# Sixteen attention units: a loop with a fixed body replaced by one written-out order of all calls

## The chip, the core and the metric

The kernel runs on one core of one Trainium2 chip. The core has five engines with a queue each: TensorE (PE, matrix products and transposes), VectorE (DVE), ScalarE (ACT), GpSimd (POOL) and SyncE (SP), which issues all DMAs here. An engine works through its own queue in order and stops where an instruction waits for another engine. The metric is device microseconds (us) of one execution; lower is better. Times below are medians of repeated runs, and one more execution was profiled.

## The reference

Three parts follow each other. (a) A linear attention with decay over B=4 batches, H=8 heads, 768 tokens and head size 48. (b) A soft mixture of experts (MoE) over all 3072 tokens. (c) A feed-forward network (FFN) with squared relu.

```python
for t in range(S):
    kt, vt, rt = (k[:, :, t], v[:, :, t], r[:, :, t])
    cur = np.einsum('bhd,bhe->bhde', u[None] * kt, vt)
    y[:, :, t] = np.einsum('bhd,bhde->bhe', rt, state + cur)
    state = w[None, :, :, None] * state + np.einsum('bhd,bhe->bhde', kt, vt)
...
logits = x @ phi                       # 3072 tokens, 8 experts x 4 slots
d = softmax over tokens of logits;  c = softmax over slots of logits
slot_input = d.T @ x                   # then per expert relu(. @ w1[e]) @ w2[e]
x = c @ slot_out
...
h = x @ w_in;  out = maximum(h, 0)**2 @ w_out     # 384 -> 2048 -> 384
```

## The kernel before

The attention is cut into 16 units n: batch b = n//4 and two heads of it. A unit holds 768 tokens as six chunks of 128, handled by parity (`par`, three even and three odd chunks). Its data come in one DMA (`load_unit`, L88) into one of five slots of SBUF. All calls are Python functions that issue a handful of instructions; a manual schedule keeps them in the order written, so the order of the calls is the order in each engine's queue. For unit n:

- `decay(n, m)` (VectorE, L236) multiplies the loaded r (m=0) or k (m=1) by powers of the decay.
- `turns(x, k)` (TensorE, L269) transposes 24 small blocks: the result of unit x back to token layout and the k of unit k. ScalarE copies both out (L266 to L276).
- `pr1` (L280), `pr2` (L284), `weigh` (VectorE, L288) and `diag(n, par)` (GpSimd, L295) make the diagonal term; `diag` writes a tile AT, of which there are three.
- `A(n, par)` (TensorE, L306): six products into two PSUM banks, one for each head. Three banks carry the tag "A"; `both` (L395, softmax transposes) and `soft3` (L446) take one of the three as well. `cp(n, par)` (VectorE, two instructions at L311) copies the two banks under a mask into AT and so frees them.
- `KV(n)` (TensorE, L318), `scan(n)` (VectorE, L322), `inter(n)` (TensorE, L336) and `intra(n, par)` (TensorE, L345) finish the unit. ScalarE copies each parity's result to a tile xT (L348), which `L(n)` (TensorE, L359) multiplies with phi.
- Per batch, softmax calls run beside later units: `soft1a` to `soft1d`, `both`, `c_max`, `c_sub` (GpSimd, L407), `c_exp`, `c_sum`, `c_div` (GpSimd, L419), `soft3`, and `soft4` (VectorE, L456). Tiles `nat` (written by `both`), `pb` (by `soft3`) and `sm` (by `c_sum`) exist once each.

Units 0 to 3 are written out by hand; units 4 to 15 run through one loop body. On TensorE the body's order is A(n,1), turns(n-1,n+2), in every fourth turn both, A(n+1,0), L(n-1), in every fourth soft3, inter(n), KV(n+1), intra(n,0), intra(n,1). The weight pieces of the MoE (24 of 512 KB, then larger ones) are issued by SyncE at the end of each turn. `keep_clock` and `filler` are products without use that keep TensorE at work in the first 13 us. After unit 15 come the last softmax steps (L686 to L727), the MoE (L743 to L783) and 96 equal steps of the FFN (L1023 the largest part); none of these is touched.

Of the kernel before, what the change touches and what calls it, by code (L numbers as in the profile page):

```python
# [17 lines left out]
def rwkv_softmoe_ffn(ctx: ExitStack, tc: tile.TileContext, un, wt, ph, w1, w2, w_in, w_out, out):  # L18
# [160 lines left out]
    def load_weight(i, cs=None):  # L179
        kind, e = W[i]  # L180
        if W[i] not in wt_of:
            t = take(home[i])
            wt_of[W[i]] = t.rearrange("p (c f) -> p c f", c=3) if kind == "w1" else t.rearrange("p (c d) -> p c d", c=8)
            st["raw", i] = t.rearrange("p (c f) -> p c f", c=3)
        t = st["raw", i]
        src = w1[e].rearrange("(c p) f -> c p f", p=128) if kind == "w1" else w2[e]
        if cs is None:
            nc.sync.dma_start(t, src.rearrange("c p f -> p c f"))
        else:
            for c in cs:  # L190
                nc.sync.dma_start(t[:, c], src[c])
# [217 lines left out]
    def c_exp(b):  # L409
        nc.scalar.activation(cnat[:, b], cnat[:, b], AF.Exp)  # L410
# [30 lines left out]
    def soft3(b, tag="A"):  # L441
        en = st["en", b]
        p = ps(tag)
        for h in range(2):
            for g in range(3):
                nc.tensor.matmul(p[32 * g:32 * g + 32, :DM + 1], en[:, h, 32 * g:32 * g + 32],  # L446
                                 xn[b % 2][:, 2 * g + h], start=(h == 0), stop=(h == 1))
        if b == 0:
            nc.scalar.copy(P2[:, 0], p[:96, :DM + 1])
        else:  # L450
            st["pb"] = wk([96, DM + 1], "pb", 1)
            nc.scalar.activation(st["pb"], p[:96, :DM + 1], AF.Copy, scale=st["f", b][1])
# [97 lines left out]
    intra(0, 1)  # L550
    rk(2)
    UT_of()
    A(1, 1)
# [12 lines left out]
    decay(3, 0)
    intra(1, 0)
    pr1(4)
    KV(2)
    intra(1, 1)  # L570
    scan(2)
    load_next(1)
    L(0)
    turns(0, 3)
    decay(4, 1)
    pr2(3)
    A(2, 0)
# [23 lines left out]
    pr2(4)
    intra(3, 0)
    decay(5, 0)
    cp(3, 1)
    KV(4)
    weigh(4)
    intra(3, 1)
    load_next(3)
    decay(6, 1)
    diag(4, 0)  # L610
    pr2(5)
    cp(4, 0)
    diag(4, 1)
    scan(4)
    for n in range(N0, NU):
        nxt = n + 1 < NU
        nx2 = n + 2 < NU
        nx3 = n + 3 < NU
        prev = n // NP - 1
        hp = n % NP  # L620
        if n == 7:
            sel = const.tile([128, 4, NS], F32, name="sel")
            nc.vector.reduce_sum(sel, ident.rearrange("p (q s) -> p s q", q=4).unsqueeze(1).to_broadcast([128, 4, NS, 4]), axis=AX.X)
            rm = const.tile([128, E], F32, name="rm")
            nc.vector.reduce_sum(rm, ident.rearrange("p (q e j) -> p e q j", q=4, e=E), axis=AX.XY)
            ones = const.tile([1, 4], F32, name="ones")
            nc.gpsimd.memset(ones, 1.0)
        A(n, 1)
        if prev >= 0 and hp == 2:
            c_exp(prev)  # L630
        if nx2:
            pr1(n + 2)
        if nxt:
            weigh(n + 1)
            diag(n + 1, 0)
        cp(n, 1)
        if prev >= 0 and hp == 2:
            c_sum(prev)
        if n > 0 or nx2:
            turns(n - 1 if n > 0 else None, n + 2 if nx2 else None)  # L640
        if prev >= 0 and hp == 1:
            both(prev)
            soft1d(prev)
        if nx2:
            pr2(n + 2)
        if nx3:
            decay(n + 3, 1)
        if nxt:
# [4 lines left out]
        if prev >= 0 and hp == 2:
            soft3(prev)
        if prev >= 0 and hp == 0:
            soft1a(prev)
            soft1c(prev)
        if prev >= 0 and hp == 1:
            c_max(prev)
        if nxt:  # L660
            diag(n + 1, 1)
        inter(n)
        if nxt:
            KV(n + 1)
        if nx2:
            decay(n + 2, 0)
        if nxt:
            scan(n + 1)
        intra(n, 0)
        if prev >= 0 and hp == 0:  # L670
            soft1b(prev)
        intra(n, 1)
        if prev >= 0 and hp == 1:
            c_sub(prev)
        if prev >= 0 and hp == 2:
            c_div(prev)
            soft4(prev)
        load_next(n)
        if n + NB >= NU:
            if n == NU - 2:  # L680
                load_win(0, take(NSLOT, I32))
            if n == NU - 1:
                load_weight(NSLOT)
            load_weight(NEARLY + n - NL)
# [410 lines left out]
```

## Time and profile before

| what | value |
|---|---|
| median of 3 runs | 379.99 us (379.57 to 380.36) |
| the profiled execution | 380.17 us, of which the span is 378.5 us |
| TensorE busy in the span | 368.8 us, 97% |
| VectorE, ScalarE, GpSimd busy | 266.6, 203.9, 106.6 us |
| stages | start and units to 115.2 us, softmax tail to 121.7, MoE to 154.1, FFN to 378.5 |

A busy row covers the time from an instruction's first work to its modelled end; a row of TensorE that stands on several products ("x12") can hold short waits between them, so an engine that is busy for 97% can still be waiting inside such rows. The idle time in front of a row stands in brackets with what ended it.

### The profile page before, as it was taken

How to read it: one execution, taken by the hardware profiler on the slowest of the kernel's cores; microseconds unless marked ns; L12 is line 12 of the kernel's file. 1: busy time of each engine (PE TensorE's matmuls, PEld its weight loads, DVE VectorE, ACT ScalarE, POOL GpSimd, SP SyncE). 2: the span in 40 equal slices, each digit the busy share in tenths (PEclk: the TensorE clock that was granted, in tenths of full speed). 3: DMA queues.
4: the chain of work that ended last, by engine and by line, in shares of the span. 5: the costliest groups of instructions: out<-in, count | busy, mean ns of one | idle time of the engine just before them, and what ended most of it. 6: DMA issues, size and time to landing. Idle time of an engine off the chain costs nothing.

```text
span 378.5 us, 9041 instructions
## 1 busy us (share of the span) xinstructions
PE 368.8 (97%) x3705; PEld 298.6 (79%) x3705; DVE 266.6 (70%) x460; ACT 203.9 (54%) x438; POOL 106.6 (28%) x118
## 2 busy tenths in 40 slices
PE   7999999999999999999999999999999999999995
PEld 6878878888877555888888888888888878888884
DVE  7777889999853486799876767666566756656662
ACT  2234444544532342899787856555555555555553
POOL 4765876768732131255121500000000000000000
PEclk9999999999999999999999999999999999999999
DMA  7999798998999998334232004000000120000004
GB/s 248 409 415 405 270 365 309 353 343 333 409 341 413 416 418 305 116 99 133 79 112 66 11 0 166 3 0 0 2 1 0 57 112 0 2 1 0 2 0 167
DMA packets 22281, 65.09 MB, mean 172 GB/s; under 512 B 2416, under 2 KB 4448, under 8 KB 22240
## 3 DMA queue, kind: packets, MB, share of 16 engines
q1 hardware_dynamic: 22240, 64.52, 45.2%
q8 instruction: 29, 0.48, 0.5%
q14 instruction: 12, 0.10, 0.1%
HBM read 59.00 MB, written 4.72 MB: 168 GB/s over the span
## 4 chain that ended last, share of the span: by engine, by line
PE 91%; DVE 5%; DMA 2%; ACT 1%; issue 1%; ACTq 0%; DVEq 0%
PE ps_A L1023 25%; PE ps_Y L1023 9%; PE ps_kv L1023 8%; PE ps_lg L1023 8%; PE ps_A L306 7%; PE ps_tr L928 6%; PE ps_YO L336 3%; PE ps_A L743 3%; PE ps_YE L345 3%; PE ps_Y L764 3%; PE ps_YO L345 3%; PE ps_kv L318 2%; PE ps_lg L359 2%; DVE AT L311 1%; DMA out_dram<-slot 1%; PE ps_YE L269 1%
## 5 line engine op out<-in xcount | busy, mean ns | idle before, releaser
L952 DVE TENSOR_TENSOR slot<-slot,slot 128x512 fp32r<-128x512 f32 (+1 forms) x97 | 69.5, 718 | 53.3 <-ACT slot L949 18.5
L1023 PE MATMUL ps_A<-slot,slot 128*128 128x512 f32 x432 | 105.8, 389 | 0.0
L1023 PEld LDWEIGHTS ps_A<-slot,slot 128*128 128x128 f32 x432 | 81.0, 188 | 17.1 <-ACT slot L949 0.3
L949 ACT CAST slot<-slot 128x512 fp32r<-128x512 f32 (+1 forms) x97 | 59.7, 616 | 49.9 <-DVE slot L946 49.6
L939 ACT ACTIVATE slot<-ps_tr 128x512 f32<-128x512 f32 (+1 forms) x97 | 57.4, 593 | 21.8 <-PE ps_tr L928 21.0
L946 DVE TENSOR_TENSOR slot<-slot 128x512 f32<-128x512 f32 (+1 forms) x71 | 48.4, 683 | 10.7 <-ACT slot L939 10.4
L1023 PE MATMUL ps_Y<-slot,slot 128*128 128x512 f32 x144 | 55.5, 392 | 0.2 <-ACT slot L949 0.2
L1023 PE MATMUL ps_kv<-slot,slot 128*128 128x512 f32 x144 | 55.1, 389 | 0.0
L1023 PE MATMUL ps_lg<-slot,slot 128*128 128x512 f32 x144 | 55.1, 389 | 0.0
L311 DVE COPY_PREDICATED AT<-mask,ps_A 128x384 f32<-128x384 int32 x63 | 33.6, 586 | 12.9 <-PE ps_A L306 7.9
L928 PE MATMUL ps_tr<-slot,slot 128*128 128x512 f32 x96 | 37.4, 391 | 0.4 <-DVE slot L892 0.4
L808 POOL TENSOR_TENSOR slot<-wf,slot 128x384 fp32r<-128x384 f32 x16 | 22.3, 1394 | 51.6 <-ACT slot L803 51.6
L295 POOL TENSOR_SCALAR_AFFINE_SELECT AT<-dg 128x768 f32<-128x768 f32 x32 | 28.1, 884 | 23.8 <-PE ps_YE L345 13.4
L306 PE MATMUL ps_A<-slot 48*128 48x128 f32 x378 | 33.3, 289 | 1.2 <-DVE AT L311 1.0
L1023 PEld LDWEIGHTS ps_Y<-slot,slot 128*128 128x128 f32 x144 | 27.0, 188 | 6.5 <-ACT slot L949 0.6
L1023 PEld LDWEIGHTS ps_kv<-slot,slot 128*128 128x128 f32 x144 | 27.0, 188 | 5.7
L306 PEld LDWEIGHTS ps_A<-slot 48*128 48x128 f32 x378 | 27.3, 188 | 5.2 <-DVE AT L311 2.2
L1023 PEld LDWEIGHTS ps_lg<-slot,slot 128*128 128x128 f32 x144 | 27.0, 188 | 5.5
L236 DVE TENSOR_TENSOR slot<-slot,ps_tab 112x768 f32<-112x768 f32 (+1 forms) x34 | 29.9, 891 | 1.0 <-DMA slot<-in_un_dram 1.0
L348 ACT COPY xT<-ps_YE 112x384 f32<-112x384 f32 x16 | 7.7, 480 | 30.6 <-PE ps_YE L345 30.6
L928 PEld LDWEIGHTS ps_tr<-slot,slot 128*128 128x128 f32 x96 | 17.9, 188 | 4.2 <-DVE slot L892 0.6
L284 POOL TENSOR_TENSOR slot<-slot,slot 128x576 f32<-128x576 f32 x13 | 18.4, 1417 | 7.4 <-ACT slot L276 7.1
(208 smaller groups left out, 531.4 us busy)
## 6 DMA issues: line engine op xcount, KB each, us to landing
slot<-in_un_dram SPq DMA_DIRECT2D x12, 1344.0 KB, 7.1
slot<-in_w_dram SPq DMA_DIRECT2D x24, 512.0 KB, 9.3
slot<-in_w_dram SPq DMA_DIRECT2D x8, 1536.0 KB, 10.5
slot<-in_w_in_dram SPq DMA_DIRECT2D x4, 1536.0 KB, 9.3
wo<-in_w_out_dram SPq DMA_DIRECT2D x16, 384.0 KB, 3.2
out_dram<-slot SPq DMA_DIRECT2D x18, 256.0 KB, 2.1
slot<-in_un_dram SPq DMA_DIRECT2D x9, 448.0 KB, 7.3
slot<-slot SPq DMA_DIRECT2D x48, 16.0 KB, 1.9
```

The lines of the kernel that those rows point to most:

```text
L236: nc.vector.tensor_tensor(x, x, t.unsqueeze(1).to_broadcast(list(x.shape)), ALU.mult)
L295: nc.gpsimd.affine_select(out=at, in_=dg.unsqueeze(3).to_broadcast([128, 2, HC, 128]), pattern=[[0, 2], [0, HC], [1, 128]], compare_op=ALU ...
L306: nc.tensor.matmul(p[h][:, i], tv[rows, 1, 2 * i + par], tv[rows, 0, 2 * i + par], start=True, stop=True)
L311: nc.vector.copy_predicated(st[n, "AT", par][:, h], mask.unsqueeze(1).to_broadcast([128, HC, 128]), p)
L345: nc.tensor.matmul(p[o:o + D, i], vv[:, 2 * i + par, h], at[:, h, i], start=False, stop=True, skip_group_check=True)
L808: nc.gpsimd.tensor_tensor(wout_half(wls, f, 5), st.pop(("wf", f)), hi, ALU.subtract)
L928: nc.tensor.matmul(p, gst[:, 128 * f:128 * (f + 1)], cTall[:, 512 * g:512 * (g + 1)], start=True, stop=True)
L939: nc.scalar.activation(fs[i, "hr"][:, c], fs[i, "p"][:, c], AF.Relu)
L946: nc.vector.tensor_mul(gg, hr, hr)
L949: nc.scalar.copy(part(i, "gh")[:, c], fs[i, "gg"][:, c])
L952: nc.vector.tensor_tensor(part(i, "gl")[:, c], fs[i, "gg"][:, c], fs[i, "gh"].bitcast(F32)[:, c], ALU.subtract)
L1023: nc.tensor.matmul(o, (hi, lo, hi)[k][:, 128 * j:128 * (j + 1)], (gh, gh, gl)[k], start=(f == 0 and k == 0), stop=(f == NF - 1 and k == 2))
```

## The change

The loop and the hand-written head are replaced by one list of 378 calls. The calls are the same functions on the same data with these exceptions: `keep_clock` makes six products and not seven; the copy that fills `carry` is made by ScalarE and not by GpSimd, with the two memsets that stood behind it in a call of their own; three small constants are made at unit 2 and not at unit 7; the softmax tile `pb` is remembered for each batch (there is still one buffer); and each weight piece is issued by a call of its own, in another order and at other places. Nothing is changed from `L(NU - 1)`, the logits of unit 15, on.

```diff
-            st["pb"] = wk([96, DM + 1], "pb", 1)
+            st["pb", b] = wk([96, DM + 1], "pb", 1)
...
-    keep_clock(7)
+    keep_clock(6)
...
-        nc.gpsimd.tensor_copy(carry[:, :, :, 1:], pos[:, 7].unsqueeze(2).unsqueeze(3).to_broadcast([112, NP, D, NC - 1]))
+        nc.scalar.copy(carry[:, :, :, 1:], pos[:, 7].unsqueeze(2).unsqueeze(3).to_broadcast([112, NP, D, NC - 1]))
+
+    def ones_of():
...
+    def load_piece(j):
+        load_weight(pieces[j][0], pieces[j][1:])
...
-    for n in range(N0, NU):
...
-        A(n, 1)
...
-            turns(n - 1 if n > 0 else None, n + 2 if nx2 else None)
...
-            A(n + 1, 0)
-            cp(n + 1, 0)
-        if n > 0:
-            L(n - 1)
...
+    A(7, 1)
+    turns(6, 9)
+    L(6)
+    weigh(8)
+    A(8, 0)
+    diag(8, 0)
+    inter(7)
+    intra(7, 0)
+    cp(7, 1)
+    decay(10, 1)
+    pr2(9)
+    diag(8, 1)
+    soft1c(0)
+    KV(8)
+    cp(8, 0)
...
+    both(2)
+    A(14, 0)
+    weigh(14)
+    pr1(15)
+    diag(14, 0)
+    inter(13)
+    intra(13, 0)
+    load_win(0, take(NSLOT, I32))
+    pr2(15)
+    cp(13, 1)
+    intra(13, 1)
+    cp(14, 0)
+    c_sub(1)
+    KV(14)
+    A(14, 1)
```

At the start, TensorE's queue before runs from the products of unit 0 through twelve fillers to the transposes of unit 1 (rows of the queue: line, operation, output<-inputs):

```order
L306 MATMUL ps_lg_147<-slot_1_71 128x128
L318 MATMUL ps_kv_115<-slot_1_71,slot_15_85 48x48 x10
L481 MATMUL ps_kv_115<-slot_14_84,slot_1_71 32x2 x24
L226 MATMUL ps_lg_147<-ident 128x128 x12
L269 MATMUL ps_kv_115<-ident,slot_2_72 128x48
```

The same place in the changed kernel, which has two more fillers ahead of its first transposes and two behind those of unit 1:

```order
L306 MATMUL ps_lg_147<-slot_1_71 128x128
L318 MATMUL ps_kv_115<-slot_1_71,slot_15_85 48x48 x10
L481 MATMUL ps_kv_115<-slot_14_84,slot_1_71 32x2 x24
L226 MATMUL ps_lg_147<-ident 128x128 x8
L269 MATMUL ps_kv_115<-ident,slot_2_72 128x48
```

Two of the twelve fillers now stand ahead of turns(None, 0), and A(0, 0) has moved from behind turns(None, 1) to in front of KV(0).

In the middle, TensorE's queue before has A(8,0) (L306), then L(6) (L359), then inter(7) (L336) behind the transposes of one turn:

```order
L269 MATMUL ps_kv_115<-ident,slot_5_75 128x48
L306 MATMUL ps_A_1113<-slot_4_74 128x128
L306 MATMUL ps_A_1114<-slot_4_74 128x128
L306 MATMUL ps_A_1113<-slot_4_74 128x128
L306 MATMUL ps_A_1114<-slot_4_74 128x128
L306 MATMUL ps_A_1113<-slot_4_74 128x128
L306 MATMUL ps_A_1114<-slot_4_74 128x128
L359 MATMUL ps_lg_890<-xT_1047,phs 32x128 x6
L336 MATMUL ps_YO_117<-slot_3_73,slot_15_85 48x128 x2
```

The same turn of the changed kernel:

```order
L269 MATMUL ps_kv_115<-ident,slot_5_75 128x48
L359 MATMUL ps_lg_978<-xT_1035,phs 32x128 x6
L306 MATMUL ps_A_1105<-slot_4_74 128x128
L306 MATMUL ps_A_1106<-slot_4_74 128x128
L306 MATMUL ps_A_1105<-slot_4_74 128x128
L306 MATMUL ps_A_1106<-slot_4_74 128x128
L306 MATMUL ps_A_1105<-slot_4_74 128x128
L306 MATMUL ps_A_1106<-slot_4_74 128x128
L336 MATMUL ps_YO_117<-slot_3_73,slot_15_85 48x128 x2
```

L(6) has moved from behind the A call to between the transposes and it. In nine turns of the changed order an L call stands directly between the transposes and an A call; at three places two L calls stand together.

Near the end, GpSimd's queue before has both calls of diag for unit 14 (the fourth and sixth row), the softmax subtraction c_sub of batch 2 (L407) and the diag calls of unit 15:

```order
L280 TENSOR_TENSOR slot_1_71<-slot_1_71,slot_14_84 128x576
L295 AFFINE_SELECT AT_1752<-dg_1750 128x768
L284 TENSOR_TENSOR slot_1_71<-slot_1_71,slot_15_85 128x576
L295 AFFINE_SELECT AT_1818<-dg_1750 128x768
L407 TENSOR_TENSOR cnat<-nat_1791,mx_1816 128x192
L295 AFFINE_SELECT AT_1872<-dg_1870 128x768
```

The changed kernel has c_sub of batch 1 in that place, behind pr1(15), diag(14,0) and pr2(15):

```order
L280 TENSOR_TENSOR slot_1_71<-slot_1_71,slot_14_84 128x576
L295 AFFINE_SELECT AT_1791<-dg_1788 128x768
L284 TENSOR_TENSOR slot_1_71<-slot_1_71,slot_15_85 128x576
L407 TENSOR_TENSOR cnat<-nat_1331,mx_1396 128x192
L295 AFFINE_SELECT AT_1875<-dg_1788 128x768
L295 AFFINE_SELECT AT_1961<-dg_1939 128x768
L407 TENSOR_TENSOR cnat<-nat_1778,mx_1963 128x192
```

c_sub(1), the last reader of the one `nat` tile of batch 1, is now issued after `both(2)`, whose copy by ScalarE writes the next `nat`.

## Rows read from the trace of the kernel before

**Rows 1.** The page: span, busy time by engine, chain that ended last.

```profile
span 378.5 us, 9041 instructions
PE 368.8 (97%) x3705; PEld 298.6 (79%) x3705; DVE 266.6 (70%) x460; ACT 203.9 (54%) x438; POOL 106.6 (28%) x118
...
PE 91%; DVE 5%; DMA 2%; ACT 1%; issue 1%; ACTq 0%; DVEq 0%
```

**Rows 2.** Windows: units 4 to 15, softmax tail, MoE, FFN; column heads first.

```profile
core 0: us, PE busy (x) PEld busy (x) DVE busy (x) ACT busy (x) POOL busy (x), PEclk, DMA share, GB/s
...
39.79:115.20 75.41, 74.74 (x1483) 62.82 (x1481) 62.71 (x109) 34.52 (x109) 50.24 (x50) 1.00 0.92 344
115.20:121.70 6.50, 5.78 (x90) 4.89 (x88) 3.18 (x13) 2.12 (x6) 1.19 (x3) 1.00 1.02 417
121.70:154.10 32.40, 31.82 (x415) 18.74 (x415) 20.51 (x40) 11.97 (x29) 7.00 (x11) 1.00 0.95 377
154.10:378.50 224.40, 220.06 (x1009) 180.91 (x1009) 149.63 (x241) 142.09 (x252) 22.93 (x17) 1.00 0.13 44
```

**Rows 3.** Timeline of TensorE, one unit: start, duration, tile after the arrow's names.

```profile
62.16 0.64 PE L359 MATMUL ps_lg<-xT,phs 112*32 112x128 f32 x12
62.73 0.36 PE L336 MATMUL ps_YO<-slot,slot 48*48 48x128 f32 x2
...
65.45 0.94 PE L306 MATMUL ps_A<-slot 48*128 48x128 f32 x12
66.23 0.20 PE L269 MATMUL ps_kv<-ident,slot 48*128 48x48 f32 x1
...
66.97 1.10 PE L306 MATMUL ps_A<-slot 48*128 48x128 f32 x12
```

**Rows 4.** TensorE's timeline: calls of A elsewhere, with idle time and its releaser.

```profile
26.97 1.19 PE L306 MATMUL ps_A<-slot 48*128 48x128 f32 x10 [0.52 <-DVE AT L311]
...
33.83 0.82 PE L306 MATMUL ps_A<-slot 48*128 48x128 f32 x9 [0.52 <-DVE AT L311]
...
48.00 0.94 PE L306 MATMUL ps_A<-slot 48*128 48x128 f32 x12
48.87 0.64 PE L359 MATMUL ps_lg<-xT,phs 112*32 112x128 f32 x12
...
60.81 1.42 PE L306 MATMUL ps_A<-slot 48*128 48x128 f32 x12
...
104.65 1.49 PE L306 MATMUL ps_A<-slot 48*128 48x128 f32 x12
```

**Rows 5.** Timeline of VectorE beside the row at 60.81.

```profile
58.85 1.04 DVE L623 TENSOR_REDUCE sel<-ident 128x128 f32<-128x512 f32 x1
...
60.66 1.05 DVE L311 COPY_PREDICATED AT<-mask,ps_A 128x384 f32<-128x384 int32 x2
```

**Rows 6.** Timeline of ScalarE, then TensorE, around the softmax call of unit 5.

```profile
46.09 0.49 ACT L348 COPY xT<-ps_YO 112x384 f32<-112x384 f32 x1
...
46.40 0.20 PE L269 MATMUL ps_kv<-ident,slot 48*128 48x48 f32 x1
46.63 0.26 PE L269 MATMUL ps_YO<-ident,xT 48*128 48x48 f32 x1
```

**Rows 7.** TensorE's timeline where unit 15 begins.

```profile
112.92 0.35 PE L336 MATMUL ps_YO<-slot,slot 48*48 48x128 f32 x2 [0.41 <-ACT xn L272]
```

**Rows 8.** TensorE's timeline at the start.

```profile
7.05 0.26 PE L269 MATMUL ps_kv<-ident,slot 48*128 48x48 f32 x1 [0.50 <-DVE slot L236]
...
9.83 2.94 PE L226 MATMUL ps_lg<-ident 128*128 128x128 f32 x24
```

**Rows 9.** GpSimd's groups by line and form, to 122 us.

```profile
L295 POOL TENSOR_SCALAR_AFFINE_SELECT AT<-dg 128x768 f32<-128x768 f32 x32 | 28.1, 884 | 23.8 <-PE ps_YE L345 13.4 <-DVE slot L322 5.0 <-ACT dg L483 3.9
L280 POOL TENSOR_TENSOR slot<-slot,slot 128x576 f32<-128x576 f32 x13 | 18.4, 1419 | 0.0
...
L407 POOL TENSOR_TENSOR cnat<-nat,mx 128x192 f32<-128x192 f32 x3 | 1.6, 517 | 0.0
```

More of the change, by code (lines that the diff above doesn't have):

```diff
@@ L450, in soft3 @@
         else:
-            st["pb"] = wk([96, DM + 1], "pb", 1)
-            nc.scalar.activation(st["pb"], p[:96, :DM + 1], AF.Copy, scale=st["f", b][1])
+            st["pb", b] = wk([96, DM + 1], "pb", 1)
+            nc.scalar.activation(st["pb", b], p[:96, :DM + 1], AF.Copy, scale=st["f", b][1])
     def soft4(b):
         if 0 < b < B - 1:
-            nc.vector.scalar_tensor_tensor(P2[:, 0], P2[:, 0], st["f", b][0], st["pb"], ALU.mult, ALU.add)
+            nc.vector.scalar_tensor_tensor(P2[:, 0], P2[:, 0], st["f", b][0], st["pb", b], ALU.mult, ALU.add)
     P2 = const.tile([96, 2, DM + 1], F32, name="P2")
@@ L535, in rwkv_softmoe_ffn @@
     rsc_of()
-    turns(None, 1)
-    A(0, 0)
+    filler(2)
+    decay(1, 0)
+    filler(2)
+    filler(2)
+    scan(0)
+    cp(0, 1)
+    turns(None, 1)
+    ones_of()
+    filler(2)
+    UT_of()
+    diag(0, 0)
+    cp(0, 0)
     inter(0)
-    cp(0, 1)
-    cp(0, 0)
     rk(1)
     dg_of(1)
-    diag(1, 0)
+    diag(1, 1)
+    intra(0, 0)
+    KV(1)
     decay(2, 0)
-    intra(0, 0)
     decay(2, 1)
-    diag(1, 1)
-    KV(1)
+    rk(2)
+    intra(0, 1)
+    decay(3, 1)
+    A(1, 1)
     scan(1)
[L550 to L553, printed above, removed]
+    load_piece(1)
     turns(None, 2)
     A(1, 0)
+    decay(3, 0)
     cp(1, 1)
+    diag(1, 0)
+    cp(1, 0)
+    load_unit(5)
     inter(1)
-    load_next(0)
+    KV(2)
+    scan(2)
+    pr1(3)
+    intra(1, 0)
+    constants()
+    intra(1, 1)
     dg_of(2)
-    pr1(3)
-    diag(2, 1)
     diag(2, 0)
-    decay(3, 1)
-    cp(1, 0)
+    load_unit(6)
+    A(2, 0)
+    turns(0, 3)
+    load_piece(7)
     decay(4, 0)
[L566 to L572, printed above, removed]
-    L(0)
[L574 to L577, printed above, removed]
+    L(0)
     A(2, 1)
@@ L580, in rwkv_softmoe_ffn @@
     inter(2)
+    intra(2, 0)
+    diag(2, 1)
     cp(2, 1)
+    pr2(3)
+    decay(4, 1)
+    pr1(4)
+    load_piece(5)
+    KV(3)
     weigh(3)
     diag(3, 0)
-    intra(2, 0)
-    pr1(5)
-    KV(3)
+    diag(3, 1)
     scan(3)
     intra(2, 1)
-    load_next(2)
+    pr1(5)
+    A(3, 0)
+    turns(1, 4)
     decay(5, 1)
     L(1)
-    turns(1, 4)
-    A(3, 0)
+    cp(3, 0)
+    load_piece(8)
+    pr2(4)
     A(3, 1)
     turns(2, 5)
+    load_unit(7)
+    decay(6, 0)
+    cp(3, 1)
+    L(2)
+    decay(5, 0)
@@ L596, in rwkv_softmoe_ffn @@
     A(4, 0)
-    diag(3, 1)
-    L(2)
-    cp(3, 0)
     inter(3)
[L601 to L604, printed above, removed]
     KV(4)
     weigh(4)
+    diag(4, 0)
+    decay(6, 1)
+    scan(4)
+    cp(4, 0)
+    load_piece(3)
+    intra(3, 0)
     intra(3, 1)
-    load_next(3)
-    decay(6, 1)
-    diag(4, 0)
+    A(4, 1)
+    turns(3, 6)
+    L(3)
+    soft1d(0)
     pr2(5)
-    cp(4, 0)
+    weigh(5)
     diag(4, 1)
-    scan(4)
-    for n in range(N0, NU):
[L616 to L627, printed above, removed]
-        A(n, 1)
[L629 to L639, printed above, removed]
-            turns(n - 1 if n > 0 else None, n + 2 if nx2 else None)
[L641 to L648, printed above, removed]
-            A(n + 1, 0)
-            cp(n + 1, 0)
-        if n > 0:
-            L(n - 1)
[L653 to L684, printed above, removed]
@@ new lines, in rwkv_softmoe_ffn @@
+    A(5, 0)
+    cp(4, 1)
+    load_piece(15)
+    diag(5, 0)
+    pr1(6)
+    decay(7, 1)
+    cp(5, 0)
+    pr2(6)
+    load_unit(8)
+    soft1a(0)
+    soft1b(0)
+    load_piece(4)
+    inter(4)
+    diag(5, 1)
+    decay(7, 0)
+    KV(5)
+    scan(5)
+    intra(4, 0)
+    intra(4, 1)
+    load_unit(9)
+    A(5, 1)
+    cp(5, 1)
+    turns(4, 7)
+    load_piece(17)
+    pr1(7)
+    weigh(6)
+    decay(8, 0)
+    both(0)
+    c_max(0)
+    A(6, 0)
+    inter(5)
+    intra(5, 0)
+    diag(6, 0)
@@ new lines, in rwkv_softmoe_ffn @@
+    cp(6, 0)
+    KV(6)
+    c_sub(0)
+    diag(6, 1)
+    load_piece(14)
+    pr2(7)
+    intra(5, 1)
+    load_unit(10)
+    decay(8, 1)
+    A(6, 1)
+    load_piece(2)
+    turns(5, 8)
+    load_piece(6)
+    pr1(8)
+    L(4)
+    L(5)
+    cp(6, 1)
+    weigh(7)
+    scan(6)
+    pr1(9)
+    soft3(0)
+    decay(9, 1)
+    diag(7, 0)
+    A(7, 0)
+    inter(6)
+    cp(7, 0)
+    load_piece(23)
+    intra(6, 0)
+    KV(7)
+    intra(6, 1)
+    load_unit(11)
+    pr2(8)
+    scan(7)
+    diag(7, 1)
@@ new lines, in rwkv_softmoe_ffn @@
+    A(7, 1)
[13 more added lines that the diff above has]
+    cp(8, 0)
+    decay(9, 0)
+    scan(8)
+    c_exp(0)
+    intra(7, 1)
+    decay(10, 0)
+    c_sum(0)
+    A(8, 1)
+    cp(8, 1)
+    weigh(9)
+    load_piece(16)
+    turns(7, 10)
+    load_piece(0)
+    L(7)
+    A(9, 0)
+    soft1a(1)
+    inter(8)
+    soft1b(1)
+    KV(9)
+    load_unit(12)
@@ new lines, in rwkv_softmoe_ffn @@
+    decay(11, 1)
+    load_piece(18)
+    intra(8, 0)
+    intra(8, 1)
+    scan(9)
+    KV(10)
+    pr1(10)
+    pr2(10)
+    load_piece(11)
+    diag(9, 0)
+    A(9, 1)
+    diag(9, 1)
+    cp(9, 0)
+    load_unit(13)
+    turns(8, 11)
+    both(1)
+    cp(9, 1)
+    A(10, 0)
+    inter(9)
+    pr1(11)
+    weigh(10)
+    diag(10, 0)
+    intra(9, 0)
+    diag(10, 1)
+    scan(10)
+    KV(11)
+    soft1c(1)
+    intra(9, 1)
+    A(10, 1)
+    c_max(1)
+    load_piece(12)
+    load_unit(14)
+    decay(12, 1)
@@ new lines, in rwkv_softmoe_ffn @@
+    load_piece(21)
+    cp(10, 0)
+    turns(9, 12)
+    decay(11, 0)
+    pr2(11)
+    L(8)
+    pr1(12)
+    cp(10, 1)
+    L(9)
+    A(11, 0)
+    scan(11)
+    inter(10)
+    load_piece(22)
+    intra(10, 0)
+    pr2(12)
+    intra(10, 1)
+    load_unit(15)
+    KV(12)
+    load_piece(13)
+    A(11, 1)
+    soft1d(1)
+    weigh(11)
+    diag(11, 0)
+    diag(11, 1)
+    decay(13, 1)
+    load_piece(19)
+    cp(11, 0)
+    decay(13, 0)
+    load_piece(20)
+    load_piece(9)
+    cp(11, 1)
+    load_weight(8)
@@ new lines, in rwkv_softmoe_ffn @@
+    decay(12, 0)
+    decay(14, 1)
+    turns(10, 13)
+    soft3(1)
+    c_div(0)
+    L(10)
+    pr1(13)
+    scan(12)
+    inter(11)
+    A(12, 0)
+    pr2(13)
+    intra(11, 0)
+    weigh(12)
+    diag(12, 0)
+    diag(12, 1)
+    KV(13)
+    weigh(13)
+    intra(11, 1)
+    cp(12, 0)
+    A(12, 1)
+    turns(11, 14)
+    decay(14, 0)
+    L(11)
+    cp(12, 1)
+    load_weight(9)
+    soft1a(2)
+    A(13, 0)
+    inter(12)
+    intra(12, 0)
+    pr1(14)
+    intra(12, 1)
+    soft1c(2)
+    scan(13)
@@ new lines, in rwkv_softmoe_ffn @@
+    load_weight(10)
+    A(13, 1)
+    diag(13, 0)
+    decay(15, 1)
+    soft1b(2)
+    pr2(14)
+    turns(12, 15)
+    diag(13, 1)
+    cp(13, 0)
+    both(2)
[13 more added lines that the diff above has]
+    A(14, 1)
+    turns(13, None)
+    soft1d(2)
+    load_weight(11)
+    scan(14)
+    decay(15, 0)
+    c_exp(1)
+    L(12)
@@ new lines, in rwkv_softmoe_ffn @@
+    diag(14, 1)
+    soft3(2)
+    inter(14)
+    A(15, 0)
+    intra(14, 0)
+    cp(14, 1)
+    intra(14, 1)
+    KV(15)
+    A(15, 1)
+    weigh(15)
+    soft4(0)
+    soft4(1)
+    soft4(2)
+    load_weight(13)
+    turns(14, None)
+    load_weight(12)
+    diag(15, 0)
+    c_max(2)
+    c_sub(2)
+    c_exp(2)
+    cp(15, 0)
+    diag(15, 1)
+    scan(15)
+    L(13)
+    cp(15, 1)
+    L(14)
+    c_sum(1)
+    c_div(1)
+    inter(15)
+    c_sum(2)
+    c_div(2)
+    intra(15, 0)
+    intra(15, 1)
```

44 lines of the change are left out of this document (17 added, 27 removed).

## The prediction

> **What bounds the kernel now.** I read the page first. TensorE is busy for 368.8 of 378.5 us, and the chain of work that ended last is TensorE's for 91% of the span [rows 1]. So time can only come from TensorE having less to do or waiting less. The matrix products are the same before and after, so I ask only where TensorE waits. The windows by stage say that the FFN (224.40 us) and the MoE (32.40 us) are far the larger part and that their code is untouched; the change acts in the units up to 115.20 us [rows 2]. In units 4 to 15 TensorE counts as busy for 74.74 of 75.41 us. That looks as if nothing were to be had, but a row on several products holds the short waits between them. So I went to the timeline and compared calls of the same kind.
>
> The yardstick is the unit in [rows 3]: A without a wait takes 0.94 us as a row (start 65.45), and L takes 0.57 from its start to the next call's (62.16 to 62.73). Against it, A(n+1,0) is stretched in most turns of the loop: 1.10 at 66.97 [rows 3], 1.42 at 60.81, 1.49 at 104.65, but 0.94 at 48.00 [rows 4]. A writes two of three banks, and the copy `cp` of the call before must free one. At 60.81 VectorE is seen doing just that: two copies from 60.66 to 61.71, late behind a reduction of 1.04 us that started at 58.85 [rows 5]. In units 2 and 3 two A calls follow each other with less between them, and the wait is open: 0.52 us of idle time twice, ended by the copy [rows 4].
>
> **The change, term by term.**
>
> *Start: -0.5.* TensorE stands idle for 0.50 us in front of the row at 7.05, waiting for VectorE. The twelve fillers take 2.94 us as 24 passes, 0.245 for one filler [rows 8]. Two of them move in front of this wait, where the time is lost anyway: 2 x 0.245 = 0.49. The seventh product of `keep_clock` goes from the same stretch and is worth nothing there. The copy into `carry` moves from GpSimd to ScalarE, which can have nothing to do before the transposes come at 7.05; I cost it at nothing.
>
> *Units 2 and 3: -1.5.* At 26.97 ten products take 1.19 where twelve take 0.94 without a wait, so about 0.4 more beside the idle 0.52; at 33.83 nine take 0.82 where 0.71 would be their share, 0.1 more beside 0.52 [rows 4]. In the new order A(2,0) and A(2,1) stand apart, with turns and L between them (1.3 us by [rows 3]), longer than two copies (1.05 us [rows 5]). The waits of 1.54 go.
>
> *A(n+1,0) in units 4 to 14: -2.3.* Eleven calls: five near 1.10 (0.16 each over 0.94), three at hp = 2 with 1.42 to 1.49 (0.48 to 0.55), three at 0.94 ([rows 3], [rows 4]). 5 x 0.16 + 3 x 0.5 = 2.3. In the new order L stands between the transposes and this A, 0.57 us more for the copy than before, which is above each of these waits. Also the two constants, 1.04 us of VectorE at 58.85 for the larger, have left unit 7 [rows 5].
>
> *Transposes ahead of `both`: -0.9.* In three turns `turns` waits for an xT copy which ScalarE makes behind the softmax activations: the first transposes start at 46.40, the copy ends at 46.58, and the next ones follow at 46.63 [rows 6]. That is 0.23, and the pairs behind it come more slowly; I take 0.3 in each. In the new order soft1b is issued ahead of that turn's intra calls or behind both, so that no xT copy stands behind it.
>
> *Unit 15: -0.4.* inter(15) waits 0.41 us for ScalarE's copy of the turned result [rows 7]; in the new order L(13) stands between the turned result's transposes and inter(15) beside L(14), 0.57 more [rows 3].
>
> Removed in sum: 0.5 + 1.5 + 2.3 + 0.9 + 0.4 = 5.6.
>
> *Added, other tile shapes on TensorE: +0.8.* A and the transposes share the tile 48*128, L has 112*32, inter 48*48 [rows 3]. A followed by transposes starts them 0.78 later (65.45 to 66.23); A followed by L takes 0.87 (48.00 to 48.87) [rows 4]. So I price a change of shape at about 0.1. With L between transposes and A, a turn has three changes (to L, to A, to inter) where it had two; over the whole queue, the three places with two L calls deducted, I count eight more: 0.8. The bounds are 0 and twice that, 1.6.
>
> The Trainium skill, page "TensorEngine Tiling (Array Packing)", section "Key Properties", says that changing the tiling mode drains TensorE, which speaks against this change; "TensorE: Matmul & The Clock Gate", section "Single matmul latency", gives about 175 ns for a drain. By these two pages eight changes would be an estimate of 1.4 in place of 0.8 and the result 376.8. This trace agrees that a change costs something, but shows 0.1 where A meets L.
>
> *Added, new waits: +1.0.* The same work has to be done by VectorE in a shorter time: 62.71 us in 75.41 is 83% [rows 2]; with some 4 us less it is 88%. An order that is dense for one engine leaves others less margin. I followed the new queues call by call with the durations of the trace and found no wait of TensorE that must be there, but some six places where the margin is under 0.2 us. Bounds: nothing, or as much as the A calls of the loop lost before, 2.3. I take 1.0, nearer to the lower half because the new order gives the copies more distance.
>
> *Weight pieces and unit loads: 0.* The queue of DMAs moves 344 GB/s in units 4 to 15, and 417 in the tail of softmax [rows 2]. 344 x 75.41 = 25.9 MB, which at 417 GB/s need 62.2 us; some 71 are left. So transfers have room to come earlier with the work, and what hides them is the units themselves. If they can't, see the third rival.
>
> Sum: -5.6 + 0.8 + 1.0 = -3.8. Of the profiled execution's 380.17 us (378.5 of span and 1.67 around it) that leaves 376.4; the median of the runs is 0.18 lower, so **376.2**.
>
> **Rivals.**
>
> 1. *Nearly everything is gained.* Switches near nothing and no new waits: 5.6, to 374.4, and 374.0 with waits of the same kind that are too small for the list. For it: the loop's order was the same for all turns, whatever softmax call came in, and a free order can fit each one. Against: A to L shows 0.1 for a change of shape.
>
> 2. *Half is given back: VectorE takes over.* Where a call of VectorE comes late by half a copy, A waits 0.25 to 0.35 in each of twelve units, 3.0 to 4.2 in place of 1.0: 378.2 to 379.2, or 377.5 where only eight units do so. For it: VectorE at 88%, and `cp` always in the chain from A to A. Against: 0.57 more distance.
>
> 3. *The transfers hold.* If the unit loads or the weights of the MoE don't arrive earlier, TensorE waits for them in the units or at the MoE, whose DMA share is 0.95 already [rows 2]. Then what the units gain is lost there, and the time stays at 379.3 to 380.5. Against: the room of some 9 us worked out above.
>
> 4. *Slower: GpSimd's queue holds the last softmax.* c_sub(1) now stands behind pr1(15) (1.42), diag(14,0) (0.88), pr2(15) (a product of pr1's shape, 1.42) and takes 0.52 itself [rows 9]: 4.24. ScalarE's copy for both(2) waits for it, because there is one `nat`; with 0.48 for a copy of this size, as xT's [rows 6], the bank of both(2) comes free 4.7 after GpSimd could start on pr1(15). TensorE needs this bank for A(14,1), after A(14,0), inter, intra and KV: 0.87 + 2.72 (62.73 to 65.45 in [rows 3]) = 3.6 after both(2). So it idles for 1.1 + d, where d is how long after both(2) pr1(15) starts. Following the queues I get d near -1.8: no wait. Everything else on ScalarE, the xT copies too, stands behind this copy, so each us here is a us of TensorE. It takes the whole gain and another 0.8 from 1.1 + d = 4.6, d = 3.5 on: 381 or more. For it: GpSimd was never so full at the end of a batch; against: it needs some 5 us of delay that I can't find.
>
> **Chances.** The forecast (375.2 to 377.2) 0.50; nearly everything 0.16; half given back 0.18; transfers hold 0.06; slower 0.10. What a measurement of this kernel can tell from no change is about 0.2%, 0.76 us: faster is below 379.23, and the first three cases lie there, 0.84; the third rival is the same, 0.06; the fourth slower, 0.10. The range reaches from the whole gain, 374.0, to the end of the second rival, 379.2, and leaves out the last two cases.
>
> **What the changed profile would show.** Right: L(15) starts about 3.8 us earlier than the 115.20 at which the tail of softmax begins [rows 2]; MoE and FFN keep 32.4 and 224.4 us; the rows of A are 0.94 nearly everywhere; VectorE's share up to L(15) rises by some 5 points; rows of idle time in front of A named DVE AT are gone in units 2 and 3. The switch term is right if A still starts some 0.1 later behind L than behind transposes. Wrong: the MoE stage grows by what the units lose (third rival); rows at both(2) to A(14,1) with idle time ended by ScalarE's `nat` (fourth); rows of A over 1.1 us through the middle, with two copies of VectorE across their start (second). The prediction would be wrong too if a load of a unit (rows of decay with idle time ended by a DMA) came late, which I cost at nothing.

## The result: 376.05 us

The changed kernel takes 376.05 us (median of 5 runs, 375.92 to 377.63) against 379.99 before; the ratio is 0.9907 (0.9885 to 0.9929). The forecast was 376.2. The profiled execution took 376.01 us. Medians here and below leave out the few executions that were over 1.5% above the fastest of their kernel. Its page, as in [rows 1]:

```profile
span 374.3 us, 9041 instructions
PE 366.4 (98%) x3703; PEld 298.7 (80%) x3703; DVE 266.6 (71%) x460; ACT 205.4 (55%) x439; POOL 103.7 (28%) x117
...
PE 97%; DVE 1%; issue 1%; ACT 0%; POOL 0%; POOLq 0%; ACTq 0%
```

TensorE's share of the chain rose from 91 to 97%, and VectorE's fell from 5 to 1%: the chain hardly runs through VectorE any more. The windows, cut at the same calls as [rows 2] (columns as there; the first one is the start up to the transposes of unit 2):

```profile
0.00:19.09 19.09, 17.01 (x280) 14.62 (x282) 16.01 (x36) 6.11 (x16) 9.59 (x25) 1.00 0.90 338
...
38.16:111.22 73.06, 73.06 (x1483) 62.97 (x1481) 59.82 (x107) 34.65 (x109) 50.32 (x49) 1.00 0.98 374
111.22:117.72 6.50, 5.77 (x90) 4.89 (x88) 3.18 (x13) 2.12 (x6) 1.60 (x4) 1.00 1.01 407
117.72:149.90 32.18, 31.60 (x415) 18.73 (x415) 20.27 (x40) 11.74 (x28) 7.16 (x11) 1.00 0.95 366
149.90:374.30 224.40, 220.01 (x1010) 181.02 (x1009) 150.75 (x241) 142.72 (x253) 21.24 (x17) 1.00 0.13 43
```

A(4,1) to L(15) took 75.41 us and takes 73.06, and the start of the units is 1.8 us shorter: before it was 20.90 (18.89 to 39.79), now 19.07 (19.09 to 38.16). L(15) begins at 111.22, 3.98 earlier than at 115.20. The tail of softmax (6.50) and the FFN (224.40) are equal to the hundredth, the MoE is 0.22 shorter. The very first stage lost 0.2, from 18.89 to 19.09.

A turn in the middle, TensorE's timeline, to be held against [rows 3] and the row 60.81 of [rows 4]:

```profile
57.58 0.94 PE L306 MATMUL ps_A<-slot 48*128 48x128 f32 x12
58.35 0.20 PE L269 MATMUL ps_kv<-ident,slot 48*128 48x48 f32 x1
...
59.24 0.64 PE L359 MATMUL ps_lg<-xT,phs 112*32 112x128 f32 x12
59.81 0.94 PE L306 MATMUL ps_A<-slot 48*128 48x128 f32 x12
60.68 0.35 PE L336 MATMUL ps_YO<-slot,slot 48*48 48x128 f32 x2
```

A(7,1), transposes, L(6), A(8,0), inter(7): A takes 0.94 both times, without a wait. The transposes last 0.89 (58.35 to 59.24) where they lasted 0.74 ahead of A. In units 2 and 3, where [rows 4] shows 0.52 us of idle time twice, the A calls now stand as single rows of 0.94:

```profile
24.10 0.94 PE L306 MATMUL ps_A<-slot 48*128 48x128 f32 x12
...
25.77 0.64 PE L359 MATMUL ps_lg<-xT,phs 112*32 112x128 f32 x12
26.34 0.94 PE L306 MATMUL ps_A<-slot 48*128 48x128 f32 x12
...
29.94 0.94 PE L306 MATMUL ps_A<-slot 48*128 48x128 f32 x12
...
32.13 0.94 PE L306 MATMUL ps_A<-slot 48*128 48x128 f32 x12
```

The start has a wait that was not forecast, in the products of dg_of(1):

```profile
15.34 0.56 PE L481 MATMUL ps_kv<-slot,slot 112*32 112x2 f32 x46
16.27 0.22 PE L481 MATMUL ps_kv<-slot,slot 112*32 112x2 f32 x2 [0.36 <-issue]
```

"issue" says that TensorE waited for nothing that the profile shows. What this is became the second question of the experiments.

At the end of batch 2 the chain of the fourth rival is there, with no loss. GpSimd first, then ScalarE's copy for both(2) and TensorE's A(14,1):

```profile
94.62 1.42 POOL L280 TENSOR_TENSOR slot<-slot,slot 128x576 f32<-128x576 f32 x1
95.99 0.88 POOL L295 TENSOR_SCALAR_AFFINE_SELECT AT<-dg 128x768 f32<-128x768 f32 x1
97.45 1.42 POOL L284 TENSOR_TENSOR slot<-slot,slot 128x576 f32<-128x576 f32 x1 [0.58 <-ACT slot L276]
98.81 0.52 POOL L407 TENSOR_TENSOR cnat<-nat,mx 128x192 f32<-128x192 f32 x1
```

```profile
99.36 0.48 ACT L397 COPY nat<-ps_A 128x384 f32<-128x384 f32 x1 [2.06 <-POOL cnat L407]
...
100.03 0.94 PE L306 MATMUL ps_A<-slot 48*128 48x128 f32 x12
```

pr1(15) starts at 94.62, 1.8 ahead of the end of both(2) at 96.44: the d of -1.8 that the forecast rests on. c_sub(1) ends at 99.33, the copy at 99.84, and TensorE needs the bank at 100.03. The margin was 0.19. (In the listing of GpSimd's queue before, the two calls of diag for unit 14 are the second and the fourth row; the sixth belongs to unit 15.)

### The profile page after: what moved, and what is told of

It is laid out like the page before. It is cut to its first block, busy times and chain, and to the rows that moved or that the text cites. A ratio compares the mean times of both kernels' runs of the same rounds, so it can differ in the third digit from the quotient of the medians.

```text
span 374.3 us, 9041 instructions
## 1 busy us (share of the span) xinstructions
PE 366.4 (98%) x3703; PEld 298.7 (80%) x3703; DVE 266.6 (71%) x460; ACT 205.4 (55%) x439; POOL 103.7 (28%) x117
## 4 chain that ended last, share of the span: by engine, by line
PE 97%; DVE 1%; issue 1%; ACT 0%; POOL 0%; POOLq 0%; ACTq 0%
PE ps_A L1229 26%; PE ps_Y L1229 9%; PE ps_kv L1229 9%; PE ps_lg L1229 9%; PE ps_A L306 7%; PE ps_tr L1134 6%; PE ps_YO L336 3%; PE ps_YE L345 3%; PE ps_A L949 3%; PE ps_YO L345 3%; PE ps_Y L970 3%; PE ps_lg L359 2%; PE ps_kv L318 2%; PE ps_YE L269 2%; PE ps_lg L222 1%; PE ps_kv L269 1%
## 5 line engine op out<-in xcount | busy, mean ns | idle before, releaser
L1158 DVE TENSOR_TENSOR slot<-slot,slot 128x512 fp32r<-128x512 f32 (+1 forms) x97 | 71.1, 734 | 53.5 <-PE ps_A L1229 18.6
L1014 POOL TENSOR_TENSOR slot<-wf,slot 128x384 fp32r<-128x384 f32 x16 | 20.6, 1288 | 53.2 <-ACT slot L1009 53.2
L306 PE MATMUL ps_A<-slot 48*128 48x128 f32 x378 | 30.3, 288 | 0.0
L306 PEld LDWEIGHTS ps_A<-slot 48*128 48x128 f32 x378 | 24.5, 187 | 4.9 <-issue 3.2
```

Source lines behind the costliest of these rows:

```text
L1014: nc.gpsimd.tensor_tensor(wout_half(wls, f, 5), st.pop(("wf", f)), hi, ALU.subtract)
L1158: nc.vector.tensor_tensor(part(i, "gl")[:, c], fs[i, "gg"][:, c], fs[i, "gh"].bitcast(F32)[:, c], ALU.subtract)
```

## The experiments

Medians swing by some tenths from chip to chip (the kernel before: 379.99, 380.35 and 380.29 in the three sets; the changed kernel again: 376.64, ratio 0.9914, 0.988 to 0.9948). So they can't settle an edit that is worth some tenths: of the variants of the changed kernel that follow, only a_calls_adjacent and pieces_and_fewer_fillers have an interval that does not overlap 0.9885 to 0.9929, and both reach into that of the repeat. Beside each median stands the start of L(15) in the one profiled execution. The same kernel differs there too: the changed kernel, profiled again (**changed_again**), has L(15) at 111.73 and not at 111.22. It was expected to stop in dg_of(1) for 0.3 to 0.5 us or not at all; its largest stop named issue stands within the transposes of units 2 and 5:

```profile
33.62 0.20 PE L269 MATMUL ps_kv<-ident,slot 48*128 48x48 f32 x1 [0.30 <-issue]
```

The start of the program alone makes some 0.4 us of difference.

### What freed A: distance on TensorE, or VectorE's order?

**l_behind_a**: the changed kernel, ten L calls moved back.

```diff
     turns(6, 9)
-    L(6)
     weigh(8)
     A(8, 0)
+    L(6)
```

> The changed kernel with the ten early L calls of units 0 to 9 and unit 11 put back behind the A call that follows them; VectorE's, ScalarE's and GpSimd's orders stay. Theory of the prediction (the 0.57 us of L between transposes and A is what lets the copy free a bank): the A calls wait again by 0.1 to 0.7 us each at nine places, 1.9 in all, while the transposes lose the 0.15 us by which they last longer in front of L (0.89 against 0.74), 1.35 in all: 376.05 becomes about 376.6. Rival (the copies are early because VectorE's order is new, and L between them and A only costs tile changes): A waits almost nowhere and the time falls by up to 1.3, to about 374.8.

377.35 us, ratio 0.9947 (0.9918 to 0.9976); L(15) at 111.92, 0.70 later, with 0.4 less in the stage of the start. All calls of A together take 2.02 more in TensorE's timeline, where 1.9 was expected; the transposes take 0.97 less, 1.35 less but for a stop of 0.38 in one of them, of the kind treated below. The largest wait is in front of A(9,0):

```profile
63.51 0.94 PE L306 MATMUL ps_A<-slot 48*128 48x128 f32 x12
...
65.03 0.45 PE L306 MATMUL ps_A<-slot 48*128 48x128 f32 x2
65.85 0.93 PE L306 MATMUL ps_A<-slot 48*128 48x128 f32 x10 [0.37 <-DVE AT L311]
66.71 0.64 PE L359 MATMUL ps_lg<-xT,phs 112*32 112x128 f32 x12
```

At only two of the nine places does A lose clearly more than the tile change saves (0.45 in front of A(2,1) and 0.71 in front of A(9,0); transposes, A and L together take 0.31 and 0.56 more). At five the two cancel to within 0.02, and at A(4,0) and A(5,0) the kernel is 0.13 and 0.07 faster with L behind A. L in front of A is a gain only where the copy is late. The medians, 0.9947 against 0.9907 with overlapping intervals, show the direction at most; the rows carry this.

**l_ahead_in_loop**: the kernel before, one edit.

```diff
+        if n > 0:
+            L(n - 1)
         if nxt:
             A(n + 1, 0)
             cp(n + 1, 0)
-        if n > 0:
-            L(n - 1)
```

> The kernel before, with one edit in its loop: L(n-1) stands ahead of A(n+1,0). Theory of the prediction: the waits of A in units 4 to 14 (2.3 us) go, the transposes become 0.15 longer in eleven turns (1.65), and the time falls by some 0.6, to 379.4. Rival (VectorE's order counts): the copy is still late by the weighing in front of it, of the 2.3 only a part goes, and the tile changes make the kernel equal or up to 1 us slower, 380 to 381.

379.45 us (378.95 to 383.69), ratio 1.0002 (0.9979 to 1.0026): in time not to be told from no change. In the profile L(15) starts at 114.25, 0.95 earlier. A takes 2.37 us less over the whole queue, the transposes 1.14 more. The row that took 1.42 [rows 4] takes 0.94 here, behind L:

```profile
59.36 0.94 PE L306 MATMUL ps_A<-slot 48*128 48x128 f32 x12
...
60.98 0.64 PE L359 MATMUL ps_lg<-xT,phs 112*32 112x128 f32 x12
61.55 0.94 PE L306 MATMUL ps_A<-slot 48*128 48x128 f32 x12
```

**copy_ahead_in_loop**: the kernel before, VectorE's order alone.

```diff
+        cp(n, 1)
         if nxt:
             weigh(n + 1)
             diag(n + 1, 0)
-        cp(n, 1)
```

> The kernel before, with one edit in its loop: cp(n,1) stands ahead of weigh(n+1) and diag(n+1,0), so that VectorE's copy of the banks comes 0.73 us earlier. Rival theory (VectorE's order removes the waits of A): the 2.3 us of waits in units 4 to 14 go without any tile change, and the time falls by about 2, to 378. Theory of the prediction (distance on TensorE by L): the wait only moves to the next copy, since weigh and diag of the next unit come later, and no more than 0.7 is gained, 379.3 to 380.

379.69 us, ratio 0.9989 (0.9976 to 1.0001); L(15) at 115.02, 0.18 earlier, though the transposes of unit 2 start 0.27 later (19.16 against 18.89): the units are 0.45 shorter. At unit 7 the copy stands directly behind the constants, 0.14 earlier than in [rows 5], and A still waits:

```profile
59.38 1.03 DVE L623 TENSOR_REDUCE sel<-ident 128x128 f32<-128x512 f32 x1
...
60.52 1.05 DVE L311 COPY_PREDICATED AT<-mask,ps_A 128x384 f32<-128x384 int32 x2
...
60.83 1.26 PE L306 MATMUL ps_A<-slot 48*128 48x128 f32 x12
```

Two of the three long waits of A(n+1,0) became 0.16 and 0.30 shorter (rows of 1.26 here and 1.13 at 86.49); the other nine calls are as before. So one swap on VectorE frees some 0.45 of A's 2.3 us, and one swap on TensorE frees all of it and pays more than half back in tile changes. In the profiles the theory of the prediction holds for the loop; in the times neither kernel can be told from the one before. Other orders of VectorE in the loop were not tried.

### Units 2 and 3, and softmax

**a_calls_adjacent**: the changed kernel with the pairs of A calls of units 2 and 3 together.

```diff
-    A(2, 0)
     turns(0, 3)
...
     L(0)
+    A(2, 0)
     A(2, 1)
```

> The changed kernel with A(2,0) put directly ahead of A(2,1), and A(3,0) with its copy directly ahead of A(3,1), as in the kernel before. Theory of the prediction: the second A call of each pair waits for the copy again, 1.1 and 0.5 us, 1.6 in all, and the tile changes stay; the time rises to about 377.6. Rival (units 2 and 3 have slack further on): TensorE catches up and the time stays near 376.

379.19 us, ratio 0.9962 (0.9945 to 0.9978); L(15) at 113.90. A takes 1.53 more, as expected, and the late copies make VectorE late for the next transposes, 0.46 more:

```profile
27.72 0.93 PE L306 MATMUL ps_A<-slot 48*128 48x128 f32 x10 [0.53 <-DVE AT L311]
...
31.84 0.26 PE L269 MATMUL ps_kv<-ident,slot 48*128 48x48 f32 x1 [0.46 <-DVE slot L322]
```

Nothing is caught up. The loss is larger than the A calls alone.

**softmax_behind_copy**: soft1b of three batches put back between the two xT copies.

```diff
-    soft1b(0)
...
     intra(4, 0)
+    soft1b(0)
     intra(4, 1)
```

> The changed kernel with soft1b of batches 0 to 2 put back between the two xT copies of its turn. Theory of the prediction: the transposes ahead of both wait again, by about 0.2 to 0.3 in each of three turns, 0.6 to 0.9 in all, 376.7 to 377. Rival: the xT copy has slack in the new order, no change.

376.33 us, ratio 0.9891 (0.9871 to 0.9911): no change that can be measured. In the profile the wait of [rows 6] comes back in two of three turns, 0.2 each:

```profile
43.70 0.47 ACT L370 ACTIVATE el<-ps_lg,nmx 96x256 f32<-96x256 f32 x1
...
44.32 0.49 ACT L348 COPY xT<-ps_YO 112x384 f32<-112x384 f32 x1
...
44.63 0.20 PE L269 MATMUL ps_kv<-ident,slot 48*128 48x48 f32 x1
44.86 0.26 PE L269 MATMUL ps_YO<-ident,xT 48*128 48x48 f32 x1
```

This term is real in its place and was sized too high: the edit brings back 0.4, and 0.9 was forecast.

### The stops named issue

**pieces_as_before**: the weight pieces in the order and at the units of before.

```diff
-    load_piece(10)
+    load_piece(0)
+    load_piece(1)
+    load_piece(2)
...
     load_unit(5)
+    load_piece(3)
+    load_piece(4)
```

> The changed kernel with the 24 weight pieces issued in the order and at the units of the kernel before (behind the unit loads). Theory of the prediction: transfers are hidden, no change, 375.7 to 376.5. Rival (the new spread of the pieces lets the unit loads or the weights of the MoE come in time): a decay or the MoE waits for a DMA and 1 to 4 us of the gain are lost.

377.2 us, ratio 0.992 (0.9899 to 0.994), an interval that overlaps that of the changed kernel; L(15) at 112.63, 1.41 later than in the first profile of the changed kernel and 0.90 later than in the second. Neither theory named what happened: no product of the MoE waits for a DMA, and one decay does, for 0.30 at 33.32, with no wait of TensorE for VectorE in the units; but inter(2) stops:

```profile
26.80 0.28 PE L306 MATMUL ps_A<-slot 48*128 48x128 f32 x2
28.17 0.35 PE L336 MATMUL ps_YO<-slot,slot 48*48 48x128 f32 x2 [1.09 <-issue]
```

In the DMA view of 25.6 to 27.0 us, where the data queue is full, stands one packet of the queue for instructions:

```profile
q1 hardware_dynamic: 157, 0.56, 98.9%
q8 instruction: 1, 0.02, 4.3%
```

The page counts 29 such packets and 0.48 MB, 16 KB each. Counted over TensorE's rows (weight loads, products and semaphores, the first one being 0), the stop is in front of row 961 and the packet ends 1.42 us before it; the stop in dg_of(1) above is in front of row 449, 1.46 us behind the end of a packet; a third one here is at row 1217, 1.49 behind. The rows differ by 256 or a multiple. The new theory: TensorE's own instructions come by DMA in blocks of 256 and TensorE stops where a block is late. All of the units' loss against the first profile lies at three places, of which two are these stops (1.10 and 0.44) and the third is 0.07 of A.

**five_fillers_fewer** and **pieces_and_fewer_fillers**: twenty TensorE rows taken out ahead of all this, in the changed kernel and in the one above.

```diff
-    filler(2)
+    filler(1)
     turns(None, 0)
...
-    filler(2)
     rsc_of()
-    filler(2)
```

> The changed kernel with seven fillers and not twelve: one ahead of the first transposes, four behind dg_of(0), two behind the next transposes. Theory A (the fillers are on the path of the start): 4 x 0.245 behind dg_of(0) and 0.15 ahead of the transposes go, turns(2) starts 1.1 earlier than at 19.09, and the time falls to about 375. Theory B (the path of the start is the products of GpSimd and the copies of VectorE): TensorE waits for them instead, dg_of(1) until 14.6 and intra until 14.3, and turns(2) is at most 0.3 earlier. Of the idle 0.36 us named issue in dg_of(1): if it is TensorE's instructions that come late, it stays at the same number of instructions from the start, some 20 instructions later in the program, and at the same time, 16.3.

> The changed kernel with the weight pieces at the places of the kernel before (377.2, with an idle time of 1.09 us named issue in front of inter(2), about 969 TensorE rows from the start, and 0.29 within turns(2,5)) and five fillers fewer, which takes 20 TensorE rows out. Theory (TensorE's own instructions come by DMA in packets of 16 KB and come late where the queue of data is full): the idle time stays about 969 rows from the start, so it moves out of the front of inter(2) to some ten products behind it, and ends some 1.45 us after a packet of the instruction queue. Rival (inter(2) waits for data that the profile does not show): it stays in front of inter(2).

pieces_and_fewer_fillers: 378.5 us, ratio 0.995 (0.9931 to 0.9968). The stop has left the front of inter(2) and stands within it, ten products (twenty rows) later in the program and again in front of row 961, as the theory of late instructions expected (a further one of 0.93 stands in front of row 3009); its rival is out:

```profile
27.14 0.38 PE L336 MATMUL ps_YO<-slot,slot 48*48 48x128 f32 x2
28.50 0.35 PE L336 MATMUL ps_YO<-slot,slot 48*48 48x128 f32 x1 [0.98 <-issue]
```

five_fillers_fewer: 377.39 us, ratio 0.9934 (0.9912 to 0.9956), not faster than the changed kernel as theory A had it, and probably slower; the intervals overlap. Its profiled execution (378.91, 1.5 above this median) reaches the transposes of unit 2 at 18.31, 0.78 earlier than 19.09, and then loses it: stops in front of rows 449, 1217, 1473, 1729, 2753, 3009 and 3265, each 449 plus a multiple of 256. TensorE's waits in the units that are named issue:

```profile
PE ps_YE L269 <- issue: 1.4, 3, 1.0
...
PE ps_A L306 <- issue: 0.5, 1, 0.5
...
PE ps_kv L269 <- issue: 0.4, 1, 0.4
```

L(15) is at 114.06. The fillers were on the path of the start, as theory A had it, but in this execution the stops took back more than the start had gained.

**pieces_at_end** and **pieces_at_end_fewer_fillers**: all 24 pieces issued behind unit 15, so that the MoE waits for its weights; only the units are read.

```diff
-    load_piece(10)
...
+    for j in range(24):
+        load_piece(j)
     L(NU - 1)
```

> The changed kernel with all 24 weight pieces issued behind unit 15, so that the units run with a third of the transfers gone; the MoE then waits for its weights and the total is some 25 us longer, which says nothing. Read only up to L(15). Theory (TensorE's instructions come late where the data queue is full): the packets of the instruction queue lie further ahead, no idle time named issue is left in the units, and L(15) starts at 110.6 to 111.1. Rival (those stops have nothing to do with transfers): the same stop in dg_of(1).

> The changed kernel with seven fillers and all 24 weight pieces behind unit 15; read only up to L(15). Theory (transfers delay TensorE's instructions): without them none of the stops at rows 449 + 256 k is left that made the kernel with seven fillers reach L(15) at 114.06, and L(15) starts at 109.8 to 110.8. Rival (with fewer fillers TensorE runs into waits for other engines): L(15) stays at 112 or later.

The single executions take 401.03 and 402.01 us. With seven fillers L(15) comes at 111.51 and not at 114.06, and of the 2.3 us of waits named issue one of 0.4 is left in that view:

```profile
PE ps_kv L269 <- issue: 0.4, 1, 0.4
```

With twelve fillers L(15) comes at 111.17, against 111.22; the stop in dg_of(1) is still there (0.22), at a time when the data queue is full without the pieces too (101% of its share from 13 to 16 us), and one of 0.19 stands in front of row 1985. So L(15) comes 2.55 us earlier without the pieces in the one pair of kernels, and next to nothing earlier in the other. That transfers lengthen the stops fits the first pair, but it is not shown: these are single executions, the one with 2.3 us of stops took 1.5 us more than the median of its kernel, and the second pair disagrees. Both of my numbers (109.8 to 110.8, and 110.6 to 111.1) were too low. Taking the pieces away does not end all stops, and the 0.4 that is left does not account for all of the miss with seven fillers.

### The small edits

**small_edits_undone**: `carry` on GpSimd, seven products in keep_clock, constants at unit 7.

```diff
-    keep_clock(6)
+    keep_clock(7)
...
+    constants()
     A(7, 1)
```

> The changed kernel with the copy into carry back on GpSimd behind rk(0), seven products in keep_clock, and the small constants made at unit 7 again. Theory of the prediction: carry and keep_clock are worth nothing, the constants (1.04 and 0.28 us of VectorE) make the copies of unit 7 late and cost up to 0.5, so 376 to 376.8. Rival (VectorE is full in the middle and these edits carry much of the gain): 377.5 or more.

376.9 us, ratio 0.9907 (0.9886 to 0.9928), beside 376.64 and 0.9914 for the changed kernel in the same set: no difference that can be measured. The three together are not where the gain comes from.

## Why the prediction was right

The mechanism held: TensorE's waits for banks and copies fell away, tile changes and small new waits took a part back. The size of the whole held better than its terms. By its own steps, with sums over TensorE's timeline of the one profiled execution of each kernel:

- *Units 2 and 3, -1.5*: measured -1.9 over the five A calls. The forecast had left out the third wait of the stretch (0.33). a_calls_adjacent brings 1.53 of it back.
- *A(n+1,0), -2.3*: measured -2.2 over the eleven calls; A takes 4.2 less in all, 1.9 of that in units 2 and 3. l_ahead_in_loop gains 2.3 in the same eleven calls by L alone.
- *Transposes ahead of both, -0.9*: too large. Those calls take 1.00, 0.89 and 0.90 now where they took 1.12, so -0.57, and softmax_behind_copy brings back 0.4.
- *Unit 15, -0.4*: measured -0.5, from L(14) to inter(15), 1.05 before and 0.54 now.
- *Tile changes, +0.8*: about right as a sum, wrong in its place. A behind L starts with no loss (0.57 from 59.24 to 59.81), and inter behind A costs what L behind A did (0.87 both times). It is the transposes ahead of L that last 0.15 longer. Over the units that is some 1.2, less 0.33 at the three pairs of L calls: 0.9. The Trainium skill's drain of about 175 ns ("TensorE: Matmul & The Clock Gate", "Single matmul latency") is near the 0.15 at this one change; two of the three changes in a turn cost nothing more than before.
- *New waits, +1.0*: about 0.5 in the units, none of them over 0.14.
- *Start, -0.5*: this step failed. "Two of them move in front of this wait, where the time is lost anyway" is true of the order, but the first transposes start at 7.20 and not at 7.05, and dg_of(1) takes 1.08 where it takes 0.51 without its stop. The stage lost 0.2. The late instructions are not all of it: in softmax_behind_copy, whose start is the same, the first transposes start at 6.57 and dg_of(1) has no stop, and the stage still ends at 18.78, 0.1 earlier than before; there TensorE waits for VectorE ahead of its first two calls of transposes, 0.4 and 0.3. The five kernels with this start end the stage between 18.69 and 19.10, the three with the start of before between 18.89 and 19.16, so no gain is shown.
- *Weight pieces, 0*: the transfers did come earlier (374 GB/s in the units, 344 before), and the third rival did not come. But "hidden" was too simple: in its profile pieces_as_before loses 0.9 to 1.4 us, at stops in front of blocks of TensorE's instructions; its median is higher by 0.6 to 1.2 us, with overlapping intervals.

The errors at the start (0.7) and at both (0.3) were made up for by units 2 and 3 (0.4), smaller new waits (0.5) and 0.2 in the MoE. That these cancel is luck: 376.2 lies nearer to 376.05 than the terms deserve. A slip in the second rival changes nothing: 4.2 us of waits in place of 1.0 give 376.2 + 3.2 = 379.4 and not 379.2. Also wrong: VectorE's share in units 4 to 15 was to rise by five points; it is 59.82 of 73.06, 82% (83% before). The two constants (1.3 us) have left this stretch, and soft4 takes 0.61 and 0.62 where it took 1.24 once and 0.59.

## What to carry to other kernels

A row on many products hides waits: compare rows of the same call before believing that an engine with 99% is full. A call that needs a buffer freed by another engine was helped here by an independent call of the same engine in front of it, and each such move should be weighed against the 0.15 us of a tile change, place by place, as only two of nine clearly paid here. Once an engine's data waits are gone, look at idle time named issue, and count the engine's rows in front of it: the same remainder each time says that its instructions came late. Profile a kernel twice before reading such a stop as the cost of an edit.

## What the runs showed of the hardware

TensorE's instructions come by DMA in packets of 16 KB on a queue of their own, 256 rows each: 29 packets for the 7456 to 7483 rows of every one of the fourteen traces. In the profiled executions, stops of 0.2 to 1.1 us (smaller ones beside them) stood in front of rows 449, 961, 1217, 1473, 1729, 1985, 2753, 3009 and 3265, in no kernel all of them, and where a stop was over 0.2 it ended 1.2 to 1.5 us after a packet's end. The Trainium skill, "Runtime: NRT & Kernel Launch", section "Instruction fetch mechanics", has the block of 256 and calls its cost mostly hidden; the block agrees with these rows, and in units of some 6 us with some 250 rows each the cost is not hidden here. If the first packet belongs to row 449 and each next one to 256 rows later, packets start 33 to 294 rows ahead of the row that needs them. In the units, each stop of 0.2 us or more named issue stands where that lead was 33 to 78 rows, apart from those in front of row 449; at some leads of 69 to 79 rows there is none of this size. The kernel before has a lead as short as 48 rows too, in front of row 961, but there TensorE stands waiting for VectorE at that time ([rows 4], 26.97), and it has no stop named issue of over 0.15 us. What sets the moment at which a packet is sent stays open: in five_fillers_fewer one started at 76.55 while the data queue was at a quarter of its share.
